# Halved transform tables turned on chip, earlier raw weights, filters copied inside DRAM, and tail regroupings on three queues

## The chip, the cores and the metric

The kernel runs on one core of a Trainium2 chip. The metric is the device time of one execution in microseconds. All arithmetic is 32-bit float, apart from the bit work that turns the 64-bit weights into 32-bit ones.

In the text, TensorE is PE in the profile, VectorE is DVE, ScalarE is ACT, GpSimd is POOL and SyncE is SP. SP, ScalarE and GpSimd each issue DMAs from their own instruction stream, in order: a DMA issue that must wait holds all that stands behind it in that stream.

## What is computed

```
X = rfft(x, axis=1)                      # x: 8 entries of 3136 x 256
y = irfft(X * (filt_r + 1j * filt_i))    # a filter per frequency and channel
h = y.reshape(25088, 256) @ w_in         # 256 x 1024
solu = h * softmax(h)
ln = (solu - mean) / sqrt(var + 1e-6) * g_ln
out = ln @ w_out                         # 1024 x 256
```

The sequence of 3136 is taken as 49 x 64, so that each transform is a product with a 49-point table, a twiddled 64-point one, and the same two backwards after the filter.

## The kernel before

**Stages of one entry.** `first` multiplies pieces of x by the 49-point table and stores the result to a DRAM tensor `d1` (d<-x in the profile). When all pieces of an entry are stored, its *spectrum* runs in 7 units (`units`; each holds two pairs of residues, the last holds one): fetch from `d1` (t<-d), `forward` (product with the "there" half of the table `de`), `multiply` by the filter in two parts, `inverse` (product with the "back" half of `de`), and `store` to `d2` (d<-g). Then `back` or `back_halves` fetches from `d2` and writes `y`, which lies in SBUF and holds two entries. Of `de`, the back half of each pair of residues is the 128 x 128 transpose of its there half; both lie in the DRAM table `de_dram`.

**The start** does the first entry (e = 0) alone. `load_tables` brings 13 tables `de` and 13 filters in three groups: pairs 0 to 3 and 4 to 7 from GpSimd's queue, 8 to 12 from SP's. `start(i)` runs `forward` of a unit, two units ahead of `multiply` and `inverse`. Fillers (`idle`, `idle_row`) are products whose result nobody reads; they keep TensorE running while it waits. The weights come as raw 64-bit words: `begin(j)` issues the load of raw half-block j (0 to 7, 512 KB each, five buffers) from GpSimd's queue, and `convert(j)` (lines 420 to 451) rebuilds floats on VectorE with help from ScalarE and GpSimd. `weight_sums` forms the four differences (L149) that the seven-product form of a 2 x 2 matrix product needs. Lastly the filters of the first entry are written from SBUF to `f_dram` (L596, four DMAs on SP) for the later entries, and x of the second entry is fetched into unused room of `y`.

**The main loop** is `step(k)`, k = 0 to 204. A step is one block of 128 tokens of the dense part; two steps are a pair j, since products run in groups of seven over a pair (`product`, L728; `project`, L859). The second product of a pair runs LAG = 9 steps later. Between lie `finish` (sum and minimum, on VectorE), `exponential`, `normalize` (L776), `square`, `turn` (a 32 x 32 block transpose on VectorE) and `regroup` (L809): DMAs that gather the turned blocks into solu_t, four of 128 KB for one block of 128 tokens. `project_sums` (L707) forms on GpSimd the sums of solu_t that the seven products need, and `pair_sums` those of y. `keep_out` (L875) and `finish_out` (L879) write the output tile.

Beside this, the step carries work of the later entries by lists of jobs, filled ahead by the times in `PLAN`: `first_parts`, `second_parts`, `top`, `early`, `middle`, `late`, `stores`, `products` and `loads`. The second entry (e = 1, object `second`) has its pieces in steps 0 and 1 and its spectrum units in steps 4, 5, 6, 7, 8, 10 and 12; the third entry's pieces come from step 5 on, its spectrum from step 18. For these, `fetch_quarters` loads x (L249, SP's queue), `difference` (L258, VectorE) and `sum` (L264, GpSimd) prepare it, `first_quarters` (L273) multiplies, and `store_quarters` (L284, GpSimd's queue) stores. `load_filter` (L647) loads a unit's filter from `f_dram` on GpSimd's queue, one DMA per unit; a unit's two filter buffers alternate with one in the unused room of `y`. The order of jobs inside a step is the order in which each engine meets them:

```python
for job in top[k] + stores[k] + products[k]:
    job()
...
for job in late[k] + loads[k]:
    job()
if k < 2:
    for n in ((0, 1), range(2, 7))[k]:
        prepare_w_out(n)
```

`prepare_w_out` scales w_out by g_ln (step 0, L665), forms its mean over rows with TensorE (step 1, L673), subtracts it (step 2, L678), and forms the four differences of w_out (steps 3 to 6, L149, on GpSimd).

Of the kernel before, what the change touches and what calls it, by code (L numbers as in the profile page):

```python
# [94 lines left out]
def kernel(  # L95
# [15 lines left out]
    wb_dram = nc.inline_tensor(wb_host, name="wb_tbl").ap()  # L111
    de_dram = nc.inline_tensor(de_host, name="de_tbl").ap()
    rows = np.arange(P)[:, None]
    turn_dram = nc.inline_tensor(np.concatenate(
# [291 lines left out]
    with ExitStack() as st:  # L406
# [62 lines left out]
        def load_tables(i0, n, dma):  # L469
            de = fpool.tile([P, n, 2, 2, NQ], FP32, name=f"de_{i0}", tag=f"de{i0}")  # L470
            dma(out=de, in_=de_dram[i0:i0 + n].rearrange("i p k u q -> p i (k u q)"))
            f = fpool.tile([P, n, 2, C], FP32, name=f"f_{i0}", tag=f"f{i0}")
            for place, k, held, rows in all_filter_rows(i0, n):
                dma(out=f[place, 0:held, k, :], in_=rows)
            for i in range(n):
                tables[i0 + i], filters[i0 + i] = (de, i), (f, i)

        weights = []
# [36 lines left out]
        st.enter_context(tc.manual_schedule())  # L515
        nc.sync.dma_start(out=wf_t, in_=wf_dram)
        pieces = NH // NCH

# [50 lines left out]
        for i in range(2):  # L569
            start(i)  # L570
        for i in range(units):
            if i + 2 < units:
                start(i + 2)
# [6 lines left out]
            if i == 0:  # L580
                nc.gpsimd.dma_start(out=wi_t, in_=wi_dram)
                nc.gpsimd.dma_start(out=wq_t, in_=wq_dram)
                nc.gpsimd.dma_start(out=wb_t[:, 0:N1], in_=wb_dram)
                nc.gpsimd.dma_start(out=g_sb, in_=moe_g_ln.rearrange("(k p) -> p k", p=P))
            elif i != 2:
                begin({1: 2, 3: 3, 4: 4, 5: 5, 6: 6}[i])
        idle_row(14, "idler")
        rows_t4 = pools["r"].tile([P, NH, C], FP32, name="t4_0", tag="r")
# [4 lines left out]
        fetch_second()  # L593
        for i0, n, rows in ((0, 4, P), (4, 4, P), (8, NP - 9, P), (NP - 1, 1, NQ)):
            f, at = filters[i0]
            nc.sync.dma_start(  # L596
                out=f_dram[i0:i0 + n].rearrange("i u q k c -> (u q) i (k c)")[0:rows],
                in_=f[0:rows, at:at + n].rearrange("p i k c -> p i (k c)"))
        convert(2)
        begin(7)  # L600
        convert(3)
        convert(4)
        weight_sums(w_in_sb)
        for j in (5, 6, 7):
# [38 lines left out]
    def load_filter(sp, u):  # L643
        i, pairs = sp.units[u]
        f = sp.buffer(u, "f", [P, 2, 2, C])
        rows = NQ if i == NP - 1 else P
        nc.gpsimd.dma_start(  # L647
# [6 lines left out]
    def prepare_w_out(step):  # L654
# [27 lines left out]
        else:  # L682
            weight_sum(nc.gpsimd, w_out_sb, step - 3)

# [197 lines left out]
    def store_out(p):  # L882
# [11 lines left out]

    (top, early, middle, late, stores, loads, products, first_parts, second_parts, spectrum_loads) = (
        [[] for _ in range(blocks + LAG + 1)] for _ in range(10))

# [5 lines left out]
    for e in range(1, B):  # L903
# [5 lines left out]
        for i, t in enumerate(first_at):  # L909
# [10 lines left out]
            else:  # L920

                row_loads.append((t, t - 2, -1, lambda sp=sp, i=i: sp.fetch_quarters(i, nc.sync.dma_start)))
                stores[t].append(lambda sp=sp, i=i: sp.difference(i))
                products[t].append(lambda sp=sp, i=i: sp.sum(i))
# [23 lines left out]
        for ch, t in enumerate(back_at):  # L948
# [4 lines left out]
                e, ch, [psum(f"py_{e}_{ch}_{g}") for g in range(2)]))  # L953
            (late if second_one else middle)[t].append(lambda e=e, ch=ch: join_halves(e, ch))
    row_loads.sort(key=lambda load: load[0])
    for n, (t, latest, earliest, load) in enumerate(row_loads):
# [11 lines left out]
    def step(k):  # L968
# [7 lines left out]
        if k < LAG:  # L976
# [5 lines left out]
            else:  # L982
                product(j, 5)
                keep(j, k - 1, 1)
                finish(j, k, 1, (k - 1, 1), 2)
        for job in top[k] + stores[k] + products[k]:
            job()
# [4 lines left out]
        if not odd:  # L992
# [35 lines left out]
            for job in spectrum_loads[k]:  # L1028
                job()
            if 0 <= j - 3 < pairs - 1:  # L1030
                for n in range(j - 3, pairs if j - 3 == pairs - 2 else j - 2):
                    regroup(n, 0)
                    if n != last[-1]:
                        regroup(n, 1)
            if 0 <= j - 4 < pairs:
                project_sums(j - 4, 1)
            if 0 <= j - 3 < pairs and j % 2:
                deviations((j - 3) // 2)
# [13 lines left out]
        else:  # L1052
# [6 lines left out]
            if proj:  # L1059
                project(p, 1)  # L1060
                keep_out(p, 0, (0, 0))
            if j == pairs + 1:
                regroup(last[-1], 1, nc.scalar.dma_start, range(2))
            if proj:
                project(p, 2)
                finish_out(p, 0, 0, (0, 0), 1)
# [17 lines left out]
            if proj:  # L1084
                keep_out(p, 1, (1, 0))
            if j == pairs + 1:
                regroup(last[-1], 1, nc.scalar.dma_start, range(2, 4))
            if 3 <= k < blocks + 3:
                square(k - 3)
            for job in first_parts[k]:  # L1090
                job()
        for job in late[k] + loads[k]:
            job()
        if k < 2:
            for n in ((0, 1), range(2, 7))[k]:
                prepare_w_out(n)

# [37 lines left out]
```

## Time and profile before

| | us |
|---|---|
| median of 3 runs | 1616.96 (1612.08 to 1617.99) |
| profiled execution, its own time | 1613.62 |
| span of that execution | 1611.60 |
| PE busy | 1554.8 (96%) |
| DVE busy | 1321.1 (82%) |
| POOL busy | 1189.6 (74%) |
| ACT busy | 912.1 (57%) |
| mean granted TensorE clock | 0.992 of full speed |
| DMA moved | 311.93 MB, mean 194 GB/s |

The span runs from the first to the last instruction of the profiled execution; the execution's own time lies 2.0 us above it. In the views that follow, a line of the timeline gives the start in us, the length in us, the engine (PEld is the load of weights into TensorE; a q behind an engine's name is its queue, so SPq is a DMA issue on SP), the line of the kernel, the operation, out<-in with the shapes, a count, and in brackets the idle time ahead of it with what ended it. A line of the busy time by stretch gives the stretch, its length, the busy time of each engine with its instruction count, the granted TensorE clock, the mean busy share of the 16 DMA engines, and the GB/s that they moved. In such a stretch no engine can be busier than its length; what is left over is idle time of that engine. A wait for several events is put down to the one that came last.

### The profile page before, as it was taken

The numbers are of one execution on the slowest core, as the hardware profiler recorded it, in microseconds if no ns is written. First come the engines' busy times: TensorE is split into PE (matmuls) and PEld (weight loads), VectorE is DVE, ScalarE is ACT, GpSimd is POOL, SyncE is SP. The second block draws the span as 40 slices with busy tenths as digits, with TensorE's granted clock in tenths as the row PEclk, the third lists the DMA queues.
The fourth block names the chain that finished last, engine by engine and source line by source line (L and its number), as shares of the span: only waits on it lengthen the run. The fifth ranks groups of instructions, "written<-read, shape, count | busy, mean of one in ns | idle before, by whom it ended". The sixth has DMA issues, their size and how long they took to land. (4 is left out here: it accounts for less than half of the span.)

```text
span 1611.6 us, 37022 instructions
## 1 busy us (share of the span) xinstructions
PE 1554.8 (96%) x12808; PEld 1058.1 (66%) x12808; DVE 1321.1 (82%) x2635; ACT 912.1 (57%) x1821; POOL 1189.6 (74%) x1378
## 2 busy tenths in 40 slices
PE   5898899999999999999999999999999999999997
PEld 1363466666666676667766676667766777777777
DVE  1687897898899889987999889887998777777773
ACT  2135565565656656566565655566555656666662
POOL 4446987679787977896779877697776866677774
PEclk8999999999999999999999999999999999999999
DMA  9887968787798678766887679766784554343443
GB/s 269 255 278 235 282 195 220 219 231 196 219 260 225 184 202 259 220 188 167 231 238 205 168 194 253 194 184 182 199 239 134 130 129 125 96 112 101 112 110 105
DMA packets 342555, 311.93 MB, mean 194 GB/s; under 512 B 28058, under 2 KB 308147, under 8 KB 342371
## 3 DMA queue, kind: packets, MB, share of 16 engines
q1 hardware_dynamic: 268692, 167.89, 39.6%
q0 software_dynamic: 34496, 101.70, 21.0%
q10 hardware_dynamic: 39184, 39.98, 8.1%
q8 instruction: 104, 1.70, 0.5%
q14 instruction: 79, 0.65, 0.1%
HBM read 124.78 MB, written 81.40 MB: 128 GB/s over the span
## 5 line engine op out<-in xcount | busy, mean ns | idle before, releaser
L859 PEld LDWEIGHTS o<-w_out_sb,solu_t 128*128 128x128 f32 x3136 | 383.5, 193 | 53.2 <-issue 43.5
L859 PE MATMUL o<-w_out_sb,solu_t 128*128 128x128 f32 x3136 | 403.7, 277 | 6.0 <-DVE ot L879 5.2
L728 PE MATMUL m<-w_in_sb,s 128*128 128x512 f32 x784 | 399.2, 610 | 4.8 <-ACT h L738 3.3
L859 PEld LDWEIGHTS o<-w_out_sb,u 128*128 128x128 f32 x2352 | 306.2, 192 | 139.4 <-issue 105.9
L776 DVE SCALAR_TENSOR_TENSOR h<-e,rsum,h 128x1024 f32<-128x1024 f32 x196 | 324.3, 1655 | 6.9
L859 PE MATMUL o<-w_out_sb,u 128*128 128x128 f32 x2352 | 310.4, 275 | 2.4 <-ACT ot L875 2.3
L728 PE MATMUL m<-w_in_sb,y 128*128 128x512 f32 x588 | 306.7, 605 | 3.0 <-DVE h L749 2.0
L738 ACT COPY h<-m 128x512 f32<-128x512 f32 x294 | 172.9, 588 | 207.1 <-PE m L728 194.4
L875 ACT ACTIVATE ot<-o,rs_t 128x128 f32<-128x128 f32 x392 | 143.0, 366 | 250.1 <-PE o L859 239.8
L707 POOL TENSOR_TENSOR u<-solu_t 128x512 f32<-128x512 f32 x98 | 138.2, 1410 | 187.5 <-DMA solu_t<-turn 129.1
L784 ACT ACTIVATE h<-h,nmu 128x1024 f32<-128x1024 f32 x196 | 224.8, 1147 | 48.3 <-DVE turn L792 38.4
L792 DVE STREAM_TRANSPOSE turn<-h 128x1024 f32<-128x1024 f32 x196 | 243.1, 1240 | 3.1
L752 DVE CUSTOM_DVE_ANT_0 h<-m,h 128x512 f32<-128x512 f32 x196 | 133.2, 680 | 126.6 <-ACT h L738 96.4
L760 ACT ACTIVATE e<-h,nmax 128x1024 f32<-128x1024 f32 x196 | 225.2, 1149 | 20.0 <-DVE h L776 18.5
L707 POOL TENSOR_TENSOR u<-solu_t,u 128x512 f32<-128x512 f32 x98 | 149.2, 1522 | 86.9 <-PE o L859 86.9
L728 PEld LDWEIGHTS m<-w_in_sb,s 128*128 128x128 f32 x784 | 128.0, 191 | 91.0 <-issue 69.4
L707 POOL TENSOR_TENSOR solu_t<-solu_t,solu_t 128x512 f32<-128x512 f32 x98 | 169.4, 1729 | 0.9
L879 DVE SCALAR_TENSOR_TENSOR ot<-o,rs_t,ot 128x128 f32<-128x128 f32 x299 | 103.6, 347 | 76.5 <-ACT ot L875 52.6
L728 PEld LDWEIGHTS m<-w_in_sb,y 128*128 128x128 f32 x588 | 96.4, 190 | 98.1 <-issue 54.6
L707 POOL TENSOR_TENSOR u<-u,solu_t 128x512 f32<-128x512 f32 x98 | 147.7, 1508 | 15.6 <-PE o L859 8.6
L707 POOL TENSOR_TENSOR s<-y 128x128 f32<-128x128 f32 x196 | 97.7, 499 | 0.5
L376 PEld LDWEIGHTS py<-wb_t,t 50*64 50x64 f32 x3584 | 58.0, 134 | 44.3 <-issue 19.4
(122 smaller groups left out, 2015.8 us busy)
## 6 DMA issues: line engine op xcount, KB each, us to landing
solu_t<-turn SPq DMA_DIRECT2D x780, 128.0 KB
out_dram<-ot SPq DMA_DIRECT2D x196, 128.0 KB
t<-d POOLq DMA_DIRECT2D x112, 200.0 KB, 7.1
d<-x POOLq DMA_DIRECT2D x100, 200.0 KB, 5.7
f<-f_dram POOLq DMA_DIRECT2D x39, 512.0 KB, 7.8
d<-g POOLq DMA_DIRECT2D x39, 512.0 KB, 5.1
t<-d ACTq DMA_DIRECT2D x37, 512.0 KB
x<-in_x_dram SPq DMA_DIRECT2D x112, 98.0 KB
```

Source lines behind the costliest of these rows:

```text
L376: nc.tensor.matmul(out=views[g][64 * h:64 * h + 64, cb, i, :], lhsT=t4[rows, i, c0:c0 + 64], rhs=wb_t[rows, 0:N1], start=True, stop=True)
L707: nc.gpsimd.tensor_tensor(out=out, in0=in0, in1=in1, op=op)
L728: nc.tensor.matmul(out=ms[j, bank], lhsT=lhsT, rhs=w_in_sb[:, w, :], start=m in (1, 2, 7), stop=True, skip_group_check=True)
L738: nc.scalar.copy(out=h_half(k, i), in_=ms[j, 0])
L752: nc.vector.tensor_tensor_reduce(out=h_half(k, i), in0=ms[j, bank], in1=h_half(*kept), scale=1.0, scalar=sofar, op0=ALU.add, op1=ALU.min, ...
L760: nc.scalar.activation(out=e, in_=hs[k], func=AFT.Exp, bias=nmaxs.pop(k)[:, 1:2], scale=-1.0, accum_out=esum)
L776: nc.vector.scalar_tensor_tensor(out=solu, in0=e, scalar=rsum, in1=solu, op0=ALU.mult, op1=ALU.mult, accum_out=nmu)
L784: nc.scalar.activation(out=solu, in_=solu, func=AFT.Square, bias=nmu, scale=-float(DFF), accum_out=variances[g][:, i:i + 1])
L792: nc.vector.transpose(out=turns[g][:, :, i, :], in_=solus[k].rearrange("p (f j) -> p f j", j=32))
L859: nc.tensor.matmul(out=pos[p, bank], lhsT=lhs[:, f, :], rhs=w[:, f, :], start=f == 0 and (m in (1, 2, 7) or alone), stop=True, skip_group_ ...
L875: nc.scalar.activation(out=out_half(p, *to)[0], in_=pos[p, 0], func=AFT.Copy, scale=rs)
L879: nc.vector.scalar_tensor_tensor(out=ot, in0=pos[p, bank], scalar=rs, in1=out_half(p, *kept)[0], op0=ALU.mult, op1=ALU.add)
```

## The change

1. **Tables.** The start loads the there half of `de` only, from a DRAM copy laid out by partition (`there_dram`), and a 128 x 128 identity (`one`). `tables_back` makes the back halves: a product with the identity for each pair, four results to a PSUM bank, and a copy by ScalarE. It runs behind `start(0)`, behind `start(1)`, and, for pairs 8 to 12, ahead of `start(4)`.
2. **Raw weights.** Raw load 2 moves from unit 1 to unit 2; 3 and 4 go together in unit 3, 5 to unit 4, 6 to unit 5; raw load 7 moves from behind `convert(2)` to behind `convert(4)`. The second filler row has 12 products in place of 14.
3. **Filters.** The four writes f_dram<-f are gone. Eight copies from the two filter inputs to `f_dram`, DRAM to DRAM on SP's queue, go into the loads of steps 6 to 13, one a step. The second entry loads its filters from the inputs themselves on SP's queue: eight DMAs of 64 KB per unit, four for the last.
4. **w_out.** All of `prepare_w_out` runs in step 0, ahead of that step's `late` and `loads`; the four differences go from GpSimd to VectorE.
5. **Order of the sums of x.** Up to step 8, `difference` and `sum` come ahead of the stores of the step; from step 9 they come behind them.
6. **Last regroupings.** Those of the last two pairs, eight DMAs for each pair, are dealt over SP, ScalarE and GpSimd in the even step in which the last turn is made; the two ScalarE groups in the odd step after it are gone.

```diff
         def load_tables(i0, n, dma):
             de = fpool.tile([P, n, 2, 2, NQ], FP32, name=f"de_{i0}", tag=f"de{i0}")
-            dma(out=de, in_=de_dram[i0:i0 + n].rearrange("i p k u q -> p i (k u q)"))
+            dma(out=de[:, :, 0].rearrange("p i u q -> p i (u q)"), in_=there_dram[:, i0:i0 + n, :])
...
+        def tables_back(i0, n):
+
+            de = tables[i0][0]
+            for first in range(0, n, 4):
+                size = min(4, n - first)
+                ps = ps_t.tile([P, 4, P], FP32, name=f"back_{i0}_{first}", tag="t")
+                for v in range(size):
+                    nc.tensor.matmul(out=ps[:, v], lhsT=de[:, first + v, 0].rearrange("p u q -> p (u q)"),
+                                     rhs=one, start=True, stop=True)
+                nc.scalar.copy(out=de[:, first:first + size, 1].rearrange("p i u q -> p i (u q)"),
+                               in_=ps[:, 0:size])
...
         nc.sync.dma_start(out=wf_t, in_=wf_dram)
+        nc.scalar.dma_start(out=one, in_=one_dram)
...
         for i in range(2):
             start(i)
+            tables_back(4 * i, 4)
         for i in range(units):
+            if i == 2:
+                tables_back(8, NP - 8)
             if i + 2 < units:
                 start(i + 2)
...
-            elif i != 2:
-                begin({1: 2, 3: 3, 4: 4, 5: 5, 6: 6}[i])
-        idle_row(14, "idler")
+            for j in {2: (2,), 3: (3, 4), 4: (5,), 5: (6,)}.get(i, ()):
+                begin(j)
+        idle_row(12, "idler")
...
-        for i0, n, rows in ((0, 4, P), (4, 4, P), (8, NP - 9, P), (NP - 1, 1, NQ)):
-            f, at = filters[i0]
-            nc.sync.dma_start(
-                out=f_dram[i0:i0 + n].rearrange("i u q k c -> (u q) i (k c)")[0:rows],
-                in_=f[0:rows, at:at + n].rearrange("p i k c -> p i (k c)"))
         convert(2)
-        begin(7)
         convert(3)
         convert(4)
+        begin(7)
...
     def load_filter(sp, u):
         i, pairs = sp.units[u]
         f = sp.buffer(u, "f", [P, 2, 2, C])
+        if sp is second:
+            for place, k, held, rows in all_filter_rows(i, pairs):
+                if held:
+                    nc.sync.dma_start(out=f[place, 0:held, k, :], in_=rows)
+            return f
...
-            weight_sum(nc.gpsimd, w_out_sb, step - 3)
+            weight_sum(nc.vector, w_out_sb, step - 3)
...
-                stores[t].append(lambda sp=sp, i=i: sp.difference(i))
+                differences[t].append(lambda sp=sp, i=i: sp.difference(i))
...
+    def copy_filter(place, k, held, rows):
+        u, q = divmod(place.start, NQ)
+        nc.sync.dma_start(out=f_dram[0:held, u, q:q + 32, k, :].rearrange("i q c -> q i c"), in_=rows)
+
+    for n, part in enumerate(all_filter_rows(0, NP)):
+        loads[LAG - 3 + n].append(lambda part=part: copy_filter(*part))
...
-        for job in top[k] + stores[k] + products[k]:
+        sums_of_x = differences[k] + products[k]
+        for job in top[k] + (sums_of_x + stores[k] if k < LAG else stores[k] + sums_of_x):
             job()
...
-            if 0 <= j - 3 < pairs - 1:
-                for n in range(j - 3, pairs if j - 3 == pairs - 2 else j - 2):
-                    regroup(n, 0)
-                    if n != last[-1]:
-                        regroup(n, 1)
+            if 0 <= j - 3 < pairs - 2:
+                regroup(j - 3, 0)
+                regroup(j - 3, 1)
+            elif j - 3 == pairs - 2:
+                regroup(j - 3, 1, nc.scalar.dma_start, range(2))
+                regroup(j - 3, 0)
+                regroup(j - 3, 1, parts=range(2, 4))
+                regroup(j - 2, 0)
+                regroup(j - 2, 1, parts=range(2))
             if 0 <= j - 4 < pairs:
                 project_sums(j - 4, 1)
+            if j - 3 == pairs - 2:
+                regroup(j - 2, 1, nc.gpsimd.dma_start, range(2, 4))
...
-            if j == pairs + 1:
-                regroup(last[-1], 1, nc.scalar.dma_start, range(2))
...
-            if j == pairs + 1:
-                regroup(last[-1], 1, nc.scalar.dma_start, range(2, 4))
...
+        if k == 0:
+            for n in range(7):
+                prepare_w_out(n)
         for job in late[k] + loads[k]:
             job()
-        if k < 2:
-            for n in ((0, 1), range(2, 7))[k]:
-                prepare_w_out(n)
```

More of the change, by code (lines that the diff above doesn't have):

```diff
@@ L112 @@
     de_dram = nc.inline_tensor(de_host, name="de_tbl").ap()
+    there_dram = nc.inline_tensor(
+        np.ascontiguousarray(de_host[:, :, 0].reshape(NP, P, P).transpose(1, 0, 2)), name="there_tbl").ap()
+    one_dram = nc.inline_tensor(np.eye(P, dtype=np.float32), name="one_tbl").ap()
     rows = np.arange(P)[:, None]
@@ L476, in load_tables @@
                 tables[i0 + i], filters[i0 + i] = (de, i), (f, i)
+        one = fpool.tile([P, P], FP32, name="one", tag="one")
+        def tables_back(i0, n):
[8 more added lines that the diff above has]
+                               in_=ps[:, 0:size])
         weights = []
@@ L891 @@
     last = range(blocks // 2 - (LAG + 1) // 2, blocks // 2)
-    (top, early, middle, late, stores, loads, products, first_parts, second_parts, spectrum_loads) = (
-        [[] for _ in range(blocks + LAG + 1)] for _ in range(10))
+    (top, early, middle, late, stores, loads, differences, products, first_parts, second_parts,
+     spectrum_loads) = ([[] for _ in range(blocks + LAG + 1)] for _ in range(11))
     def ahead(t, by):
@@ L1061, in step @@
                 keep_out(p, 0, (0, 0))
-            if j == pairs + 1:
-                regroup(last[-1], 1, nc.scalar.dma_start, range(2))
-            if proj:
                 project(p, 2)
```

## The prediction

> **What bounds the kernel now.** I read the busy time by stretch first, because a mean over the span hides where a change can act.
>
> ```profile
> core 0: us, PE busy (x) PEld busy (x) DVE busy (x) ACT busy (x) POOL busy (x), PEclk, DMA share, GB/s
> 80.00:104.00 24.00, 24.00 (x152) 18.59 (x151) 23.38 (x36) 7.97 (x16) 8.58 (x7) 1.00 0.81 240
> 104.00:132.00 28.00, 26.69 (x85) 11.41 (x83) 15.82 (x41) 13.61 (x24) 18.80 (x31) 1.00 0.85 308
> 132.00:160.00 28.00, 23.36 (x115) 8.82 (x116) 24.16 (x50) 14.59 (x27) 18.22 (x21) 1.00 0.75 229
> 160.00:184.00 24.00, 18.76 (x105) 7.56 (x102) 19.27 (x34) 12.63 (x25) 20.41 (x24) 0.96 0.90 264
> 184.00:212.00 28.00, 28.00 (x192) 17.88 (x190) 25.90 (x47) 17.62 (x35) 27.23 (x32) 0.97 0.84 252
> 212.00:1560.00 1348.00, 1336.94 (x11591) 933.54 (x11591) 1156.72 (x2323) 809.00 (x1631) 1031.40 (x1192) 1.00 0.68 186
> 1560.00:1611.60 51.60, 41.85 (x311) 37.66 (x309) 21.57 (x51) 18.59 (x44) 26.99 (x24) 0.94 0.42 112
> ```
>
> From 212 to 1560 us TensorE is busy 99.2% and sets the pace; the change touches nothing there. It can act only ahead of 212 and behind 1560. Between 104 and 212 TensorE idles 11.2 us (1.31, 4.64 and 5.24), the ceiling for a gain in the first steps; the tail idles 9.75. Next the timeline and, for the tail, the chain that ended last:
>
> ```profile
> 66.23 0.69 DVE L326 TENSOR_TENSOR pr<-pb,f 128x512 f32<-128x512 f32 x1 [4.74 <-PE pc L305]
> 130.95 5.94 POOL L149 TENSOR_TENSOR w_out_sb<-w_out_sb 128x512 f32<-128x512 f32 x4
> 132.52 3.24 DVE L776 SCALAR_TENSOR_TENSOR h<-e,rsum,h 128x1024 f32<-128x1024 f32 x1
> 154.91 0.69 DVE L326 TENSOR_TENSOR y<-pb,y 128x512 f32<-128x512 f32 x1 [2.35 <-DMA y<-f_dram]
> 181.56 0.71 PE L273 MATMUL pa<-x,wq_t 49*64 49x512 f32 x2 [2.00 <-POOL x L264]
> ```
>
> ```profile
> 1586.01 2.99 DMA solu_t<-turn
> 1589.02 0.59 ACTq L809
> 1589.66 0.38 ACT ot L875
> ```
>
> VectorE starves 4.74 us in the first entry's spectrum, at 61.5 to 66.2, because unit 4's data are late. L149 on GpSimd (5.94 us) stretches VectorE's L776 to 3.24 us; others take 1.28. A filter that comes from f_dram holds VectorE 2.35 us (and 2.17 at 173.26). TensorE waits 2.00 us for GpSimd's sum of x, which stands behind 1.85 us of store issues. In the tail a DMA issue on ScalarE's queue holds ScalarE's output work.
>
> **What the Trainium skill says.** (1) DMA: Bandwidth & Descriptors, Issuing engines are not separate DMA queues: queues of all engines run on the same 16 DMA engines and interleave. The trace agrees: one regrouping issue on SP (L809) takes 0.585 us at least and up to 3.4 us. (2) SBUF — State Buffer, SBUF: two separate sides: VectorE and GpSimd share a port pair as an exclusive lock. 1.28 against 3.24 us above agrees. (3) TensorE: Matmul & The Clock Gate, What's actually happening: an idle array falls to a lower clock. The granted clock was 0.91 in 60:80, so the stall near 61 us costs a little more than its length.
>
> **Start, to 104 us: -3.** Price of a packet: q1 moved 268,692 packets (625 B mean) in 39.6% of 16 x 1611.6 us, 38 ns each; q10 moved 39,184 (1,020 B) in 8.1%, 53 ns. The line through both gives 34 ns at 512 B. Halving the table turns 1 KB pieces into 512 B ones and saves 19 ns each: 1,024 pieces for pairs 0 to 7 give 1,024 x 19/16 = 1.2 us, 640 for pairs 8 to 12 give 0.8; the identity adds 128 x 34/16 = 0.3. Net 1.7 us less DMA ahead of unit 4. Raw load 2 (512 KB, 1.7 us of all engines by the same price) was issued at 56.49, ahead of unit 4's arrival; it moves behind unit 2, about 59.7. Ends: 1.7 if it overlaps anyway, 3.4 if not; I take 3, since VectorE's 4.74 us hole can give it.
>
> Added there: 13 transposes at 0.22 us (two records of 0.11, as L859's) are 2.9 us of TensorE; four copies of up to 0.58 (L738's row, as wide) are at most 2.3 us of ScalarE; TensorE's wait from 57.7 to 61.4 hides the last five. Those of pairs 0 to 7 lie ahead of VectorE's unbroken run from 48.15. Uncovered, they would cost 1.5 us.
>
> From 74.9 the eight-step conversions run on VectorE almost unbroken (23.38 of 24.00 us) until 110.9, so they move left as a block. Two idler products fewer free 2 x 0.86 = 1.7 us of TensorE, which I count at zero: at 111.66 TensorE waits for `finish` at 110.82, queued behind conversion 7. Raw load 7 now leaves after conversion 4's GpSimd add (about 93.5 - 3), issue 0.8, landing 5.8 to 10.6 us later by the raw rows: 97 to 102, against conversion 7's start at 104.35 - 3 = 101.4. Cost 0 to 1; I take 0.
>
> **Steps 0 to 4: -0.9.** `prepare_w_out` moves ahead of step 0's late parts. Its scaling L665 ends at 114.71 and TensorE is at the product L673 at 112.6: +2.1, because four `first` products that covered this now stand behind it. In return the subtraction L678 (2.5 us) and the four differences, now on VectorE (3.7 as those of w_in at 91.65; 2.5 undisturbed), fall into VectorE's hole 116 to 124, where it worked 0.70 of 8 us. That takes 2.5 us out of VectorE at 126.7, 2.0 of stretch at 132.52, and 5.94 out of GpSimd ahead of the sums `s` at 137.59. VectorE works 24.16 of 28 us there, TensorE idles 4.64: I take -3 of a possible -4.6, at least 0.
>
> **Steps 4 to 13: filters earlier -1.5, sums first -2, SP and DMA +3.** GpSimd loses seven loads of 0.75 us. Both waits for f_dram (4.5 us together) can go, as the second entry's filters then wait for SP only; half of it reaches TensorE, 0 to 4.5. Sums ahead of stores free TensorE's waits of 2.00 and 0.94 us at L273; I take 2, from 0 to 2.9.
>
> Against that stands SP, in order. It gains 52 filter issues; the nearest row, x of an entry (4 in 2.17 us at 134.56), makes 0.54 each: 8 ahead of unit 0's x, 16 in step 4, 16 in step 6, 8 in step 9, 4 in step 10. Eight copies of some 400 KB come in steps 6 to 13; each has 384 to 416 pieces of 1 KB, 1.4 us of the sixteen DMA engines. Steps 2 to 5 have room: SP waits 9.3 us for a turn until 159.45. From 159.45 to 212 it is nearly full, regroupings of 5.0 us stretching to 8.5 to 11.3. Between the regroupings of steps 6 and 8 come 16 x 0.54 + 2 x about 1 = 10.6 us; the first set of x in that stretch is issued at 170.5 to 174.4 and used at 183.2, and regrouping 1 ends at 189.5 and is used at 196.75. So slack of 5 to 6 us plus the 1 MB of filter loads that no longer overtakes regrouping 0. Queued behind: x for step 9, then regrouping 1, then 2 (ends 206.56, first use 211.05 on GpSimd, 219.33 on TensorE). DMA share in 156 to 212 is 0.81, and five or six copies before regrouping 3 add 7 to 8.4 of 56 us: 0.94 to 0.96, room but little. Ends 0 and +12; I take +3. The old f_dram write (3.2 MB issued at 105.5) leaves 108 to 120, where TensorE had little DMA wait (0.8 us): 0.
>
> **Tail: -1.5.** Pair 96's second block is issued by 1586.4 on SP and landed at 1589.1. Half of it moves to ScalarE's queue, free since about 1582.3, so SP ends it two issues (1.3 us) earlier; and ScalarE's two late issues (0.96 us each, holding L875 for 2.99 us) go to SP and GpSimd. GpSimd's two (0.8 each) delay `wide`, which has 5 us. The product chain of 14.7 us behind it moves by its sums: 1.3 to 3; not below 0, save if GpSimd's issues push the sums. Taken 1.5.
>
> **Sum.** -3 + 2.1 - 3 - 1.5 - 2 + 3 - 1.5 = -5.9. Against the profiled execution's own time, 1613.62 (span 1611.60 plus 2.0 around it), that is 1607.7. This execution stands 3.3 below the median shown, 1616.96; the mean of all four times is 1615.2. I put -5.9 on that mean: 1609.3, rounded 1609.
>
> **Rivals.** *All gains, SP hidden* (0.23): with SP at 0 and the wait bounds at 3.4, 4.5 and 2.9, -11 to -13, about 1603. For it: issue may cost 0.35 (the smallest x issue) rather than 0.54. Against: DMA share 0.90 in 160:184.
>
> *SP becomes the bound* (0.22), the other side: filter issues stretch like the regroupings, to 1.2 us, so 16 of them and two copies take 22 us between regroupings 0 and 1, against 6 of slack; x for step 9 comes 12 to 16 us late, TensorE stands, and nothing later returns it as it is bound from 212. +16 less the 8 to 9 of other gains: about +8, 1623; it decides when SP's extra passes some 15 us. For: the stretch seen in this stretch of time. Against: filters leave GpSimd's queue in exchange.
>
> *Not doing what it says* (0.05): raw load 7 or t<-d replaces the missing stall and the tail waits for another transfer: within 2 us of 1615.
>
> **Numbers.** Likeliest case 0.50, -2 to -9, of which 0.13 lies beyond -0.5%. Half a per cent (8 us) is about what a measurement of this kernel can tell from no change. Faster: 0.13 + 0.22 = 0.35; slower 0.18 of the SP case; the rest, 0.47, the same. Range 1600 to 1621: the all-gains case and the milder half of the SP case.
>
> **What would show it.** Right: VectorE's hole at 61 to 66 under 2 us; first product (103.85) near 100; no L149 on GpSimd ahead of 160; VectorE's waits for f_dram gone; in the tail the wait of GpSimd's sums for solu_t (3.00 at 1589.16) near 1.5 and no wait of ScalarE's L875 for its own issues. Wrong: SP without a gap from step 4 to 13 and waits for x or solu_t on VectorE, GpSimd or TensorE of over 5 us; or conversion 7 waiting for its raw load.

## The result: 1% slower, and the profile after

The kernel after takes 1629.57 us in the median of four runs (1626.41 to 1632.71), beside 1614.52 for the kernel before on the same chip: a ratio of 1.0100 with a 95% interval of 1.0080 to 1.0121, or 16 us more by the ratio (the medians lie 15 apart). The prediction had 1609, a gain of 5.9 us, and a range that ended at 1621. The profiled execution's span grew by 13.0 us, from 1611.6 to 1624.6.

First the busy time by stretch of the kernel after (columns as in the view of before; 1560 runs to the end of the span):

```profile
104.00:132.00 28.00, 28.00 (x116) 14.94 (x116) 17.20 (x42) 13.77 (x26) 16.52 (x29) 1.00 0.59 192
132.00:160.00 28.00, 23.12 (x107) 8.82 (x106) 21.53 (x47) 15.82 (x28) 10.06 (x15) 0.94 0.66 193
160.00:184.00 24.00, 15.23 (x88) 6.18 (x86) 10.97 (x22) 9.44 (x17) 11.14 (x15) 0.86 0.68 213
184.00:212.00 28.00, 24.08 (x145) 13.24 (x146) 21.88 (x39) 13.75 (x28) 20.41 (x22) 0.88 0.81 253
212.00:1560.00 1348.00, 1334.82 (x11592) 932.22 (x11592) 1151.39 (x2323) 809.33 (x1629) 1037.20 (x1198) 1.00 0.68 190
```

TensorE lost 3.5 us in 160:184 and 3.9 in 184:212 against before (18.76 and 28.00), with a lower granted clock in both (0.86 and 0.88 for 0.96 and 0.97). The mean share of the DMA engines fell there (0.68 and 0.81 for 0.90 and 0.84): they are not fuller, so bandwidth is not what ran out. The place is found by the n-th `turn` of one trace against the n-th of the other: turns 0 to 3 come 1.2 to 1.5 us later than before, turn 4 2.2, turn 5 10.9, turn 8 19.6, turns 14 to 29 about 18.2. So 17.4 us of the loss arise between turns 4 and 8, in steps 7 to 11. VectorE's timeline of the kernel after says what it waited for:

```profile
65.37 0.69 DVE L329 TENSOR_TENSOR pr<-pb,f 128x512 f32<-128x512 f32 x1 [2.74 <-PE pc L308]
...
119.14 2.50 DVE L699 TENSOR_TENSOR w_out_sb<-w_out_sb,w_bar 128x512 f32<-128x512 f32 x4 [5.04 <-ACT w_bar L696]
...
134.67 1.28 DVE L797 SCALAR_TENSOR_TENSOR h<-e,rsum,h 128x1024 f32<-128x1024 f32 x1
...
183.00 0.69 DVE L329 TENSOR_TENSOR y<-pb,y 128x512 f32<-128x512 f32 x1 [7.02 <-DMA y<-in_filt_r_dram]
184.77 0.69 DVE L330 TENSOR_TENSOR y<-pb,y 128x512 f32<-128x512 f32 x1 [1.08 <-DMA y<-in_filt_i_dram]
...
218.87 0.69 DVE L329 TENSOR_TENSOR y<-pb,y 128x512 f32<-128x512 f32 x1 [8.57 <-DMA y<-in_filt_r_dram]
```

(L329 is before's L326, L797 its L776.) The second entry's filters of units 3 and 5 hold VectorE 8.1 and 8.6 us, where a filter out of f_dram held it 2.35 us at most before. SP's own timeline of the kernel after shows why they come late; L830 is the regrouping (before L809), L665 a filter load, L978 a copy, L252 a load of x:

```profile
161.01 3.97 SPq L252 DMA_DIRECT2D x<-in_x_dram  x4
172.48 6.67 SPq L830 DMA_DIRECT2D solu_t<-turn  x8
179.20 2.02 SPq L665 DMA_DIRECT2D y<-in_filt_r_dram  x4
181.26 1.84 SPq L665 DMA_DIRECT2D y<-in_filt_i_dram  x4
183.14 1.84 SPq L665 DMA_DIRECT2D f<-in_filt_r_dram  x4
185.03 1.84 SPq L665 DMA_DIRECT2D f<-in_filt_i_dram  x4
186.91 0.59 SPq L978 DMA_DIRECT2D f_dram<-in_filt_r_dram  x1
187.60 2.13 SPq L252 DMA_DIRECT2D x<-in_x_dram  x4
189.78 0.59 SPq L978 DMA_DIRECT2D f_dram<-in_filt_r_dram  x1
190.85 11.78 SPq L252 DMA_DIRECT2D x<-in_x_dram  x4
202.67 7.94 SPq L830 DMA_DIRECT2D solu_t<-turn  x8
```

Before, SP issued the two regroupings at 159.45 and 178.29, 18.8 us apart. Now the first leaves at 172.48 (turn 3, which it waits for, was 1.5 us later, not 13), and the next 30.2 us behind it. SP came out of its earlier loads at 164.98, 4.1 us behind the end of turn 3, and then stood another 7.5 us. The filter loads take 7.7 us for 16, 0.48 each; that was foreseen. Two gaps were not: these 7.5 us, and four loads of x in 11.78 us, where others take 2.1. SP's waits in 120 to 260 us name what ended them (columns: us in total, times, longest):

```profile
SPq L252 <- DMA y<-d: 8.7, 1, 8.7
SPq L830 <- DMA t<-d: 7.4, 1, 7.4
SPq L665 <- DMA de<-de_tbl: 4.7, 1, 4.7
```

None of these issues needs what it waits for: a regrouping reads a turned block, a load of x or of a filter reads DRAM. In the program as built, each DMA of SP or ScalarE signals one of eight completion counters, dealt in turn over both engines, and waits for the DMA that had this counter before it. In the built kernel after, ScalarE's fetch `t<-d` had the counter of the regrouping's first DMA, and its fetch `y<-d` that of the second of the four loads of x; `de<-de_tbl`, the third wait, is a table that ScalarE loads, and it held filter loads at 145 us. A DMA more on SP therefore not only takes SP's time: it changes which earlier transfers SP's later issues wait for. In the trace of before the longest SP wait of this kind in 155 to 215 us is 1.9 us.

Not all of the shift reaches the end: of 18.0 us at turn 107 there are 12.9 left at turn 191. A stretch of before (TensorE's busy time second), then the stretch of after that holds nearly the same products:

```profile
1000.00:1180.00 180.00, 176.62 (x1534) 121.84 (x1533) 156.01 (x308) 107.41 (x216) 137.43 (x161) 1.00 0.73 199
```
```profile
1018.00:1194.00 176.00, 176.00 (x1538) 121.85 (x1537) 151.82 (x309) 107.94 (x217) 138.77 (x161) 1.00 0.73 204
```

Before idled 3.4 us there, after not at all: about two thirds of what was given back.

### The profile page after: what moved, and what is told of

The parts are those of the page before. It is cut to its first block, busy times and chain, and to the rows that moved or that the text cites. A ratio compares the mean times of both kernels' runs of the same rounds, so it can differ in the third digit from the quotient of the medians.

```text
span 1624.6 us, 37142 instructions
## 1 busy us (share of the span) xinstructions
PE 1558.4 (96%) x12830; PEld 1062.1 (65%) x12830; DVE 1312.4 (81%) x2639; ACT 914.9 (56%) x1825; POOL 1180.1 (73%) x1369
## 4 chain that ended last, share of the span: by engine, by line
PE 69%; DMA 2%; DVE 2%; issue 1%; POOL 0%; SPq 0%; DVEq 0%; POOLq 0%
PE o L880 31%; PE m L749 30%; PE py L379 3%; PE pc L308 2%; PE pa L276 2%; PE pb L308 2%; DMA solu_t<-turn 1%; DMA x<-in_x_dram 0%; DVE h L797 0%; PE o L844 0%; DVE h L773 0%; POOL u L728 0%; SPq L830 0%; DVE turn L813 0%; DVE ot L900 0%
## 5 line engine op out<-in xcount | busy, mean ns | idle before, releaser
L797 DVE SCALAR_TENSOR_TENSOR h<-e,rsum,h 128x1024 f32<-128x1024 f32 x196 | 320.9, 1637 | 6.9
L781 ACT ACTIVATE e<-h,nmax 128x1024 f32<-128x1024 f32 x196 | 225.1, 1149 | 18.9 <-DVE h L797 17.4
L728 POOL TENSOR_TENSOR u<-solu_t,u 128x512 f32<-128x512 f32 x98 | 145.4, 1484 | 90.0 <-PE o L880 90.0
L728 POOL TENSOR_TENSOR u<-u,solu_t 128x512 f32<-128x512 f32 x98 | 155.4, 1585 | 15.7 <-PE o L880 6.7
```

Source lines behind the costliest of these rows:

```text
L728: nc.gpsimd.tensor_tensor(out=out, in0=in0, in1=in1, op=op)
L781: nc.scalar.activation(out=e, in_=hs[k], func=AFT.Exp, bias=nmaxs.pop(k)[:, 1:2], scale=-1.0, accum_out=esum)
L797: nc.vector.scalar_tensor_tensor(out=solu, in0=e, scalar=rsum, in1=solu, op0=ALU.mult, op1=ALU.mult, accum_out=nmu)
```

## The experiments

All ratios are to the kernel before, run on the same chip in the same group of runs, with 95% intervals; its median lay between 1612.83 and 1614.07 us. One profiled execution can lie 5 or 6 us off its kernel's median (that of `h2` below took 1618.13 us with a median of 1613.28, that of `e4` 1612.48 with one of 1618.76), so sizes are taken from the ratios, and places from the traces.

**Part 3 undone in after** (`e1`, whose edit is shown), and **part 3 alone in before** (`e2`, the same edit the other way round):

```diff
+        for i0, n, rows in ((0, 4, P), (4, 4, P), (8, NP - 9, P), (NP - 1, 1, NQ)):
+            f, at = filters[i0]
+            nc.sync.dma_start(
+                out=f_dram[i0:i0 + n].rearrange("i u q k c -> (u q) i (k c)")[0:rows],
+                in_=f[0:rows, at:at + n].rearrange("p i k c -> p i (k c)"))
...
-        if sp is second:
-            for place, k, held, rows in all_filter_rows(i, pairs):
-                if held:
-                    nc.sync.dma_start(out=f[place, 0:held, k, :], in_=rows)
-            return f
...
-        loads[LAG - 3 + n].append(lambda part=part: copy_filter(*part))
```

> The kernel after with part 3 undone: the store of the filters at the start is back, the second entry's filters come as one load per region on GpSimd's queue, and nothing is copied between the filter tensors. Theory (the second entry's filters on SP cost the time): the hole of 7 us at turn 5 and of 8.6 us at turn 8 are gone, and the time is 1611 to 1614 us, 1 to 4 us below before. Rival (w_out in step 0 or the tables cost it): 1622 us or more, since turn 5 or turn 8 stay late.

> The kernel before with part 3 alone (filters from the inputs on SP for the second entry, eight copies from DRAM to DRAM, no store at the start). Theory: 1626 to 1634 us, 12 to 18 us above before, with VectorE waiting for a filter near turns 5 and 8. Rival (the loss needs the tables or w_out in step 0): within 4 us of before.

Measured: 0.9993 (0.9977 to 1.0010), and 1.0118 (1.0096 to 1.0140). Part 3 is the whole loss, 19 us alone; the other five parts together are worth -1.1 us (-3.7 to +1.6).

**Within part 3: the copies, or the loads?** After without the eight copies (`e3`), and after with the copies but the second entry's filters from f_dram by one load a unit on GpSimd (`e4`); in both the store at the start is back as in `e1`:

```diff
-        loads[LAG - 3 + n].append(lambda part=part: copy_filter(*part))            # e3
-                    nc.sync.dma_start(out=f[place, 0:held, k, :], in_=rows)        # e4
-        nc.sync.dma_start(out=f_dram[0:held, u, q:q + 32, k, :].rearrange("i q c -> q i c"), in_=rows)
+        nc.sync.dma_start(out=f_two[0:held, u, q:q + 32, k, :].rearrange("i q c -> q i c"), in_=rows)
```

> The kernel after without the eight copies from DRAM to DRAM; the store at the start is back, so that the later entries find their filters, and the second entry's filters still come from the inputs on SP. Theory: 1625 to 1631 us, within 3 us of after, with both filter waits still there. Rival (the copies, through the DMA engines or through SP, cost the time): 1611 to 1616 us.

> The kernel after with the store at the start back and the second entry's filters taken from it in one load per region on GpSimd's queue; the eight copies stay, into a DRAM tensor of their own that the later entries read. Theory: 1611 to 1617 us, the filter waits gone, the copies worth 0 to 3 us. Rival (the copies cost the time): 1626 to 1632 us.

Measured: 1.0088 (1.0056 to 1.0119), and 1.0027 (1.0011 to 1.0043). Without the copies the loss stays; without the 52 loads most of it goes. The copies are not free: `e4` lies 0.34% above `e1`, some 5 us, and its median of 1618.76 lies above the 1617 of the theory and below the 1626 of the rival. The trace of `e4` has a wait of the same kind as after, without the 52 loads (SP's waits in 120 to 260 us):

```profile
SPq L253 <- DMA y<-d: 7.4, 1, 7.4
```

L253 is its load of x; the regrouping behind it leaves at 184.59 us, 178.29 before, and from turn 7 to turn 8 it loses 6.0 us on before. So the copies' cost need not be bandwidth. What they cost in after can't be told: `e3` lies 0.1% below it, with some 0.4% of uncertainty.

**Queue, order or number of the loads?** In after, all 52 on GpSimd's queue (`f1`); on SP, but the odd units' ahead of the regrouping (`f2`); in `e1`, one load per unit on SP, 7 in place of 52 (`f3`):

```diff
-                    nc.sync.dma_start(out=f[place, 0:held, k, :], in_=rows)
+                    nc.gpsimd.dma_start(out=f[place, 0:held, k, :], in_=rows)      # f1
...
-            ahead(t, 1 if e == 1 and i % 2 == 1 else 2).append(lambda sp=sp, i=i: sp.fetch_filter(i))
+            filter_loads = spectrum_loads[(t - 1) // 2 * 2] if e == 1 and i % 2 == 1 else ahead(t, 2)   # f2
+            filter_loads.append(lambda sp=sp, i=i: sp.fetch_filter(i))
...
-        nc.gpsimd.dma_start(
+        (nc.sync if sp is second else nc.gpsimd).dma_start(                         # f3
             out=f[0:rows, 0:pairs],
```

> The kernel after with the second entry's 52 filter loads issued on GpSimd's queue and not on SP's; the copies stay. Theory (SP's place in line and its waits make the filters late): 1611 to 1618 us, no filter wait over 2 us. Rival (52 small loads from the inputs are late wherever they are issued): 1625 us or more, with VectorE still waiting 5 us or more for filters 3 and 5.

> The kernel after with the odd-numbered filters of the second entry put ahead of the regrouping in SP's order (filters 1 and 3 in the same step, filter 5 one step earlier); queue and number of loads are unchanged. Theory that the order behind the regroupings decides: the 7 us hole at turn 5 is gone, and the time is 1613 to 1620 us. Rival (the number of loads on SP, which share completion counters with ScalarE's fetches, decides): 1624 us or more, with the waits moved to other loads.

> The kernel after with part 3 undone, but with the second entry's filters on SP's queue, one load of the early copy per region (7 loads in place of 52), in the same places of SP's order. Theory that the number of SP's loads decides: 1611 to 1616 us. Rival (their place behind the regroupings decides, whatever the number): 1621 us or more, with a hole of 5 us or more at turn 5 or 8.

Measured: `f1` 1.0178 (1.0142 to 1.0213), `f2` 1.0131 (1.0102 to 1.0161), `f3` 0.9997 (0.9980 to 1.0014). My theory of the order fell with `f2`: the step from turn 4 to turn 5 lost 2.5 us and not 8.7, as it said, and the next one lost another 10.0. SP's waits of `f2` in 120 to 260 us:

```profile
SPq L665 <- DMA t<-d: 11.2, 3, 9.4
```

The filter loads themselves now stand for ScalarE's fetch. In `f1` turn 0 comes 7.2 us later than before, as late as the start of that execution ended (L699 at 125.06 us, 119.14 in after); turn 3 comes 18.8 later. Its timeline on GpSimd, and the longest of TensorE's waits in 140 to 200 us:

```profile
139.00 2.19 POOL L665 DMA_DIRECT2D f<-in_filt_r_dram  x4
141.19 2.13 POOL L665 DMA_DIRECT2D f<-in_filt_i_dram  x4
...
160.16 1.07 POOL L665 DMA_DIRECT2D f<-in_filt_r_dram  x2 [2.42 <-DMA y<-in_filt_r_dram]
```
```profile
PE pc L308 <- POOL pi L331: 23.2, 2, 11.8
```

That is 0.54 us an issue, 28 us for 52, on an engine that was 85% busy in 160:184 before. L331 is GpSimd's share of the filter products; it stands behind the loads, which run from 153.46 to 167.40 us and wait in part for one another, and TensorE waits for it. SP's queue as such is not the cause either: on both engines the 52 hold what stands behind them. With 7 loads (`f3`), the filter of unit 3 still comes 7.67 us late in the profiled execution, 5.3 us of which turn 5 shows, and yet the median time is that of before: by turn 191 that execution has given back half of its delay. The number of loads counts for more than one late filter.

**52 loads that nobody reads** (`g1`): `e1`, and where after's filter loads stand on SP, loads of 16 bytes a row into an unused tile; and **26 of them** (`h2`):

```diff
+        if sp is second:
+            for place, k, held, rows in all_filter_rows(i, pairs):
+                if held:                                  # h2: if held and k == 0
+                    nc.sync.dma_start(out=unread[place, u, k, :], in_=rows[:, 0, 0:4])
```

> The kernel after with part 3 undone, and with 52 loads of 16 bytes per row, read by nobody, where after's filter loads stand on SP. No instruction waits for their data; they only take SP's time, its order and its completion counters. Theory that the number of SP's loads is the cause: 1620 us or more, with SP's x loads or regroupings late near turns 5 and 8. Rival (the cause is that the filters themselves, 64 KB a load, arrive late): 1610 to 1616 us.

> The version with unread loads on SP, but 26 in place of 52. If SP's own time is the cause, with some 6 us of room, the loss is well under half: 1611 to 1617 us. If the waits on shared counters are the cause, they depend on which DMA meets which and not on the sum: 1613 to 1626 us, and the trace shows single waits of over 3 us on t or y.

Measured: 52 loads 1.0082 (1.0059 to 1.0104), 26 loads 1.0002 (0.9984 to 1.0021). Against `e1` the 52 cost 0.9%, some 14 us, though no instruction reads their data and they move next to nothing. So a loss of this size needs neither the bytes nor the filters' lateness: 52 more issues on SP are enough. That leaves some 5 us of part 3's 19, with about as much uncertainty, for the rest. SP's timeline with the 52 unread loads:

```profile
168.22 3.39 SPq L671 DMA_DIRECT2D unread<-in_filt_r_dram  x4
172.91 1.73 SPq L671 DMA_DIRECT2D unread<-in_filt_i_dram  x4
174.68 1.82 SPq L671 DMA_DIRECT2D unread<-in_filt_r_dram  x4
176.54 6.11 SPq L671 DMA_DIRECT2D unread<-in_filt_i_dram  x4
182.75 5.87 SPq L252 DMA_DIRECT2D x<-in_x_dram  x8
```

The eight loads of x, issued from 170.51 before, leave at 182.75, and VectorE stands for them; in its timeline:

```profile
190.64 0.69 DVE L261 TENSOR_TENSOR diff<-x 113x512 f32<-113x512 f32 x1 [11.13 <-DMA x<-in_x_dram]
```

Undisturbed, four take 1.73 us, 0.43 each and 6.9 for 16; here the 16 take 14.4. SP's longest waits of this version in 155 to 215 us name ScalarE's fetches again, for loads that need nothing on the chip:

```profile
SPq L671 <- DMA t<-d: 5.1, 1, 5.1
SPq L671 <- DMA y<-d: 4.4, 1, 4.4
```

With 26 loads the longest wait for `t`, `y` or a table in that stretch is 2.3 us. A loss of 14 us for 52 and at most 3.4 for 26, where half would be 7, is not a price per load; it begins beyond some point. 26 seem to stand close to it: the one traced execution of `h2`, the third slowest of its twelve, has eight unread loads in 9.1 us between the regroupings, and loses 10.4 us on before from turn 3 to turn 10, where `g1` loses 14.4 and `e1` 2.3.

**SP's own time, or its waits for ScalarE?** The second entry's three late fetches of `t` and `y` moved from ScalarE's queue to GpSimd's, with the 52 unread loads (`h1`), and in after (`h3`):

```diff
-            dma = nc.sync.dma_start if e == 1 and t < 8 else nc.scalar.dma_start
+            dma = (nc.scalar if e > 1 else nc.sync if t < 8 else nc.gpsimd).dma_start
```

> The version with 52 unread loads on SP, and ScalarE's three late fetches of the second entry (units 4 to 6) issued on GpSimd's queue in place of ScalarE's. Theory that SP stands because its loads wait for ScalarE's fetches on shared counters: most of the 14 us comes back, 1612 to 1618 us, and no issue on SP waits over 2 us for t or y ahead of 240 us. Rival (SP's own time for 52 issues): 1623 us or more.

> The kernel after with the same three fetches of the second entry on GpSimd's queue; the 52 filter loads and the eight copies stay on SP. Theory of the counters: 1612 to 1620 us. Rival (SP's own time, or the filters' own lateness): 1625 us or more.

Measured: `h1` 1.0053 (1.0032 to 1.0075), `h3` 1.0096 (1.0062 to 1.0130). `h1` lies 0.3% below `g1`, with overlapping intervals and in another group of runs, and `h3` where after lies. Most of the 14 us did not come back. In the trace of `h1` the waits for `t` and `y` are gone (1.7 us at most), and yet the eight loads of x leave at 183.07, as late as in `g1`, and from turn 5 to turn 10 it loses 12.7 us on before, where `g1` loses 14.6. So waits for these two fetches alone are not the loss. In their place SP's loads wait for the regroupings that had their counters before them, and for ScalarE's tables (SP's waits of `h1` in 120 to 260 us):

```profile
SPq L671 <- DMA solu_t<-turn: 6.9, 5, 3.1
SPq L671 <- DMA de<-de_tbl: 4.0, 2, 2.9
SPq L835 <- DMA de<-de_tbl: 2.8, 1, 2.8
```

Nor is the edit free: the fetch of `y`, now behind GpSimd's own work, leaves at 184.29 us, 176.02 in `g1`. SP's waits of `h3` in 120 to 260 us:

```profile
SPq L830 <- DMA de<-de_tbl: 8.4, 1, 8.4
SPq L252 <- DMA y<-de_tbl: 8.0, 2, 7.5
```

and ScalarE's timeline of the same version:

```profile
163.42 0.37 ACTq L709 DMA_DIRECT2D de<-de_tbl  x1
190.19 0.42 ACTq L709 DMA_DIRECT2D y<-de_tbl  x1
```

The same two issues of SP, a regrouping and a load of x, now wait as long for the tables of the same units, which ScalarE also loads. The wait passed from one of ScalarE's transfers to the next. So how the 14 us divide between SP's own time and waits on counters stays open; a version with all of ScalarE's loads off its queue was not tried.

**The other parts one at a time, in before.** Part 6 alone (`e5`), parts 1 and 2 (`e7`), part 5 (`e8`), part 4 (`e9`):

```diff
-                regroup(last[-1], 1, nc.scalar.dma_start, range(2))                # e5, and its pair
-        idle_row(14, "idler")                                                      # e7, with the tables
+        idle_row(12, "idler")
-        for job in top[k] + stores[k] + products[k]:                               # e8
+        for job in top[k] + (sums_of_x + stores[k] if k < LAG else stores[k] + sums_of_x):
-            weight_sum(nc.gpsimd, w_out_sb, step - 3)                              # e9, all in step 0
+            weight_sum(nc.vector, w_out_sb, step - 3)
```

> The kernel before with part 6 alone, the last two regroupings shared over three queues. From the last turn to the last instruction before took 26.6 us, the version with part 3 undone 24.5: 1.5 to 2.5 us less than before, 1611 to 1612 us. Rival (the tail is bound by TensorE, and the last regroupings are hidden): within 0.7 us of before.

> The kernel before with parts 1 and 2 alone, the turned table and the moved raw weights with two idle rows fewer. The prediction's step gave 3 us at the start: 1610 to 1612 us. The trace of after shows 0.9 us at the end of the start: 1612 to 1614 us.

> The kernel before with part 5 alone, the reordered sums of x. The prediction's step gave 2 us: 1611 to 1613 us. Rival (the sums are hidden, or their new place makes a weight sum late): no change or 1 to 2 us slower, 1613 to 1616 us.

> The kernel before with part 4 alone, w_out prepared in step 0 and its differences on VectorE. The prediction's step: -0.9 us, 1611.5 to 1613.5 us. Rival (the stall of TensorE at the mean product stays and VectorE's relief is not on the path): +1 to +3 us, 1614 to 1617 us.

Measured: `e5` 1.0001 (0.9986 to 1.0015), `e7` 0.9988 (0.9971 to 1.0004), `e8` 1.0006 (0.9985 to 1.0027), `e9` 1.0000 (0.9979 to 1.0021). None can be told from no change; `e8` speaks for its rival but doesn't exclude 2 us of gain.

**Combinations.** After with parts 3 and 4 undone, that is parts 1, 2, 5 and 6 (`e6`, and the same again as `m2`), and before with parts 1, 2 and 6 (`m1`):

```diff
-            if k == 0:
-                for n in range(7):
+            if k < 2:
+                for n in ((0, 1), range(2, 7))[k]:                                 # e6, m2; m1 also has the old sums
                     prepare_w_out(n)
```

> The kernel after with parts 3 and 4 undone: w_out is prepared as before, over steps 0 and 1 and with GpSimd's differences; tables, raw weights, order of the sums and last regroupings are those of after. If w_out in step 0 costs the 2 us that the prediction gave it and gives nothing back, this is 2 us below the version with part 3 alone undone: 1609 to 1611 us. If VectorE's relief pays for it: 1611 to 1613 us.

> The kernel before with parts 1, 2 and 6 (turned table, raw weights, last regroupings); filters, w_out and sums as before. If the gain of the version without parts 3 and 4 is real and lies at start and tail: 1609 to 1611 us, 0.2 to 0.3% below before. If it needs the sums or was noise: 1612 to 1614 us.

> The version with parts 3 and 4 undone a second time (parts 1, 2, 5 and 6 of the change). If its gain is real: 1609 to 1612 us, 0.1 to 0.4% below before. If it was noise: within 0.1% of before.

Measured: `e6` 0.9975 (0.9958 to 0.9992), `m1` 0.9978 (0.9964 to 0.9992), `m2` 1.0006 (0.9992 to 1.0020). The same program twice gave 0.9975 and 1.0006, so 0.3% from one group of runs to the next is within what this measurement does. `m1`, start and tail without the rest, is the version that came out ahead of both kernels, by 3.5 us on before and some 20 on after; after the fate of `e6` its lead over before is not taken as shown.

## Why the prediction was wrong, point by point

**What bounds it.** The reading that the change could act only ahead of 212 us and behind 1560 held: from turn 14 to turn 107 the distance to before stays within 3 us of 18. That the stretch behind 212 returns nothing did not: 5 us came back after turn 107.

**SP and DMA, taken as +3 with ends 0 and +12: this is the step that failed.** Part 3 alone measures +19, 52 unread loads +14. The price of an issue was right (0.48 measured for 0.54) and so was the count. The 5 to 6 us of room are not contradicted: 26 unread loads put 8 issues, some 3.7 us undisturbed, between the two regroupings, and their median shows no loss. Three things were wrong. The sum stopped at SP's own time and left out that an issue can wait for an earlier transfer that it doesn't need: 7.4 and 8.7 us in two places of after, where the longest such wait of before was 1.9. With a third, of 4.7 us, the loads of steps 2 to 5 did not fit into the 9.3 us of room counted for them either, and ended 4.1 us behind turn 3. How much of the 19 us these waits are is open. The copies were feared for the DMA engines (0.68 to 0.81 busy after, not 0.94) and given 1 us of SP each, while `e4` puts all eight at 5 us where nothing hides them. And moving filters off GpSimd was booked as a gain of its own.

**Filters earlier, -1.5: the sign was wrong.** The waits for f_dram (4.5 us) went, as said, and the same lines then waited 16.7 us for the inputs. That the filters "then wait for SP only" was taken for relief; SP was the engine with the least room, behind regroupings that themselves wait for turns.

**Start, -3.** The hole at 61 to 66 shrank from 4.74 to 2.74 us, not below 2; `finish(0)` at the end of the start came 0.9 us earlier (109.91 for 110.82). The first product did not come near 100: it came at 107.84, for 103.85 before, in an execution whose granted clock in 80:104 was 0.89, for 1.00. Single executions scatter as much as the step was to gain: with the same start, `e1` has a hole of 5.7 us and its first product at 102.84. Alone, parts 1 and 2 measure -1.9 us (-4.7 to +0.6): -3 is not excluded and not shown.

**w_out, -0.9.** Its pieces came as written: L699 waits 5.04 us on the mean's chain, the differences fall into VectorE's hole, L797 takes 1.28 us and not 3.24. From `finish(0)` to turn 0 the trace has 27.65 us for 25.48, but the stall of +2.1 isn't what it shows: the mean's product L694 starts at 114.82, directly behind another product. At `finish(0)` TensorE still had eight `first` products ahead (3.66 us) that it had behind it before, and it was busy 28.00 of 28 us in 104:132. TensorE set the pace there, so VectorE's freed time bought nothing until turn 0. Alone, 0.0 us within 3.4.

**Sums first, -2.** TensorE's waits for the sum of x in 100 to 1000 us fell from 5.5 us in four to 2.6 in two in after, but in the version with part 5 alone they are 5.1 in five, and the time did not move. The -2 is not seen.

**Tail, -1.5.** From the start of the last turn to the end of VectorE's last instruction: 26.98 us before, 26.34 after, 26.32 with part 6 alone, 24.83 in `e1`. ScalarE's wait for its own issues went, as said. GpSimd's wait for the last solu_t did not; in the timeline of after:

```profile
1594.57 9.64 SPq L830 DMA_DIRECT2D solu_t<-turn  x12
1594.75 1.42 ACTq L830 DMA_DIRECT2D solu_t<-turn  x2
1596.54 1.29 POOL L830 DMA_DIRECT2D solu_t<-turn  x2
...
1603.25 1.26 POOL L728 TENSOR_TENSOR u<-solu_t 128x512 f32<-128x512 f32 x1 [3.55 <-DMA solu_t<-turn]
```

SP carries 12 of the 16 in both kernels; only ScalarE's four were divided. SP took 9.64 us for its 12, for 8.24 before, and GpSimd's sum started 10.1 us behind the last turn, for 9.3 before. The two issues that SP was to be ahead by were lost in slower ones, and the step was mis-sized by that; why they were slower is not shown.

**The rivals.** "SP becomes the bound" was the right one, with 0.22 where it should have led. Its place (between the regroupings of steps 6 and 8), its sign and what would be late (x) were right, though in after the filters are late before x is. Its price was 16 us less 8 to 9 of gains. The runs give 19 and next to no gains (-1.1). Its mechanism, issues that stretch to 1.2 us, was not what happened in after: most issues took 0.46 to 0.54, and two stood 7 to 9 us. (For the rival in which all gains come, the prediction took 0.35 us as the smallest issue of x; the trace has 0.28.)

**The skill.** The lower granted clock of an idle array (TensorE: Matmul & The Clock Gate, What's actually happening) agrees with 0.86 and 0.88 in the two starved stretches; what that added was not measured by itself. The exclusive port pair of VectorE and GpSimd (SBUF — State Buffer, SBUF: two separate sides) agrees with L797's 1.28 us once GpSimd had no w_out differences; it was true and not on the path. DMA: Bandwidth & Descriptors, Issuing engines are not separate DMA queues, speaks of shared DMA engines; here the shares stayed below 0.82 in 132 to 212 us, and what shows in SP's waits is that it shares completion counters with ScalarE. That regrouping issues took 0.585 to 3.4 us, the prediction's evidence for the shared engines, does not by itself show sharing.

## What to carry over

Before many small DMAs go to an engine that issues in order, write down the issues between two that matter and the time until the second is needed: 52 more cost 14 us here, with no byte worth counting, while the medians of 26 and of 7 show no loss. Ask of each issue not only what it takes (0.43 to 0.54 us here) but which earlier transfers it has to wait for, those of the other issuing engine too; the view of waits shows it as a wait for a tile that the instruction doesn't use. A test that takes away one such wait has to look at the trace for the wait that takes its place. And what one execution's trace says of a few us has to be seen in others before it is called the change's effect.

## What was not expected of the hardware

- An issue of a small load took 0.43 us on SP with rows of 16 bytes (`g1`), 0.46 to 0.48 with rows of 1 KB (after), and 0.54 on GpSimd (`f1`): on SP the size of the rows made little difference.
- Copies of 3.2 MB from DRAM to DRAM in eight steps cost about 5 us (`e4` against `e1`), while the DMA engines of `e4` were busy 0.83 and 0.81 in 184:212 and 212:240, where most of them run; a wait of SP of 7.4 us stands among them.
- The same program measured 0.9975 and 1.0006 of before in two groups of runs, each interval leaving out the other's value.
